# The first two attention units loaded as 512 tokens, four to a partition, and the start of the kernel put in another order

## The chip, the cores and the metric

The kernel runs on one core of one Trainium2 chip. The metric is the device time of one execution in microseconds; smaller is better. Each kernel is executed several times and the median is taken.

The engines are named as the profile names them: PE is TensorE (matmul), PEld its weight loads, DVE is VectorE, ACT is ScalarE, POOL is GpSimd, SP is SyncE. SP and POOL issue most of the transfers: those of SP are described by hardware, those of POOL by software, and POOL's can convert fp32 to fp16 on the way.

## What is computed

Attention within chunks of 64 tokens, for 8 batches, 8 heads, 576 tokens and head size 64, and then a feed-forward layer over all 4608 tokens with a gate whose steepness is a parameter:

```python
scores = scale * np.matmul(q_c, k_c.transpose(0, 1, 2, 4, 3))   # chunks of 64 tokens
scores = scores - np.max(scores, axis=-1, keepdims=True)
attn = np.exp(scores)
attn = attn / (np.sum(attn, axis=-1, keepdims=True) + 1e-09)
out = np.matmul(attn, v_c)
...
h = x @ w_in                        # x: 4608 x 512, w_in: 512 x 2048
g = h * (1.0 / (1.0 + np.exp(-beta * h)))
return (g @ w_out).astype(np.float32)   # w_out: 2048 x 512
```

The inputs are fp32 and the output is 4608 x 512 fp32. The kernel computes in fp16 with fp32 sums.

## The kernel before

**Tiling.** The tokens are cut into 18 units of 256 tokens; two units make a block of 512 tokens, so there are nine blocks. Attention goes unit by unit, the feed-forward layer block by block.

**Attention of one unit.** `load_unit` (L115) loads q and k with two neighbouring tokens to a partition (`load_qk`, L88, runs of 512 bytes in memory) and v with one token to a partition (`load_v`, L108). `emit_T` (L142) transposes 32x32 squares of q and k on DVE for the first eight units; later units use a transposing transfer on SP. `emit_sc` (L209) makes the scores, transposed, into a PSUM tile of two banks from the pool `ps_s`, and takes their exp on ACT into `et`. `emit_pv` (L247) multiplies with v, to which a column of ones is attached, so that the sum of the exps comes out as column 64; its two halves s = 0, 1 (128 tokens each) go to a tile of two banks of `ps_x` and one of `ps_s`. `emit_norm` (L264) divides by that sum on DVE and gives `x16`. `emit_xt_pe` (L282) transposes x16 on PE into PSUM and copies it on ACT to `xt`, for units 0 to 5; later units use a transfer (`emit_xt_dma`).

**Feed-forward.** `emit_m` (L296) makes h for 128 of the 2048 hidden columns m: four matmuls into one bank of `ps_p` (a ring of four one-bank buffers), a tanh with beta/2 as its scale on ACT, and one instruction on DVE that gives the gated value `gt`. With the argument 256 it does half of a block's tokens. `emit_t` (L329) multiplies gt with w_out for 128 tokens, in pieces of 16 steps, copies the sum out on ACT and stores it through SP. The pools `ps_p`, `ps_s` and `ps_x` (L51 to L53) fill the eight banks: four, two and two.

**Order.** The order on each engine is the order in which the program emits instructions (`manual_schedule`, L354). Every engine works its own list in order and waits at an instruction until its operands are there.

**The start.** Unit 0 is split by heads: heads 0 to 3 (a = 0) are loaded by SP as fp32 (`raw0`) and converted on ACT (q) and DVE (k); heads 4 to 7 (a = 1) are loaded by POOL with conversion (`qk0[1]`). `emit_T_half` (L171) and `emit_sc_half` (L184) transpose and score each half; the exp stands at the end of the latter. Unit 1 takes the ordinary path: `load_qk(1)` at L367, `emit_T(1)` at L390, `emit_sc(1)` at L391. POOL issues, in this order: heads 4 to 7 of unit 0, q and k of unit 1, four tiles of v, eight groups of w_in (256 hidden columns each, L372), three of w_out, then unit 2, the last of w_out, and further units.

Between the steps `emit_idle` (L349) puts matmuls on a zero tile whose result nobody reads ("warm" in the profile): 11, 3, 13, 4, 3, 3 and 2 of them, each 512 columns wide. From L405 the layer begins for the first half of block 0 (unit 0's tokens), with the PE transposes of unit 1 between its steps; L417 does the second half (unit 1's tokens).

**Later parts that the change touches.** Units 2 and 3 are worked beside the second product of block 0 (L422 to L441), unit 4 near the end of the first product of block 1, and units 5 to 7 beside the second product of block 1 (L459 to L479). In `emit_xt_pe` the half s = 0 goes to a tile of `ps_x`; s = 1 goes to `ps_s` for unit 2 and to `ps_p` for the others.

The lines that decide where the transposes go:

```python
pool, tag = (ps_x, "x") if s == 0 else (ps_s, "s") if u == 2 else (ps_p, "p")
xp = pool.tile([128, 4, 128], FP16, tag=tag, name="xp")
```

The softmax here doesn't subtract the row's maximum and nothing guards it: scores larger than these inputs give would overflow.

## Time and profile before

| | us |
|---|---|
| median of 3 runs | 292.15 (291.8 to 292.45) |
| the profiled execution | 291.74 |
| its span, first to last instruction | 290.0 |
| PE busy in the span | 283.1 (98%) |
| PE busy with filler matmuls (39) | 11.2 |
| ACT, DVE, POOL busy | 146.0, 139.8, 97.5 |
| granted TensorE clock, mean | 1.00 |

The profiled execution lasts 1.74 us longer than its span; what lies before the first and after the last instruction is not in the span. A matmul of 512 columns in the long unbroken stretches takes 0.216 us. The matmul durations in the groups are longer (about 0.37 us), because neighbouring matmuls overlap and their ends are modelled; so the distance between starts is what counts.

In the profile's lists each line gives the start in microseconds, the duration, the engine, the line of the program, and the operation with output and input; in square brackets stands the idle time of the engine just before, and what ended it. The chain of waits follows the work that ended last back from the end, at each step to what released it. In the list of stretches each engine's busy time is followed by its number of instructions, and the last two numbers are the share of the DMA engines and the GB/s written.

The time of a transfer is given from its issue to its landing. The DMA engines are busy for over 90% of every slice from 2.5 us to about 100 us.

### The profile page before, as it was taken

To read this page: it belongs to the slowest core of one execution; us is meant where nothing else is said; L and a number is where in the kernel's file an instruction comes from. 1 tells how busy PE (TensorE), PEld (TensorE's weight loads), DVE (VectorE), ACT (ScalarE), POOL (GpSimd) and SP (SyncE) were. 2 spreads that over 40 slices of the span, in tenths; PEclk is the share of its full clock that TensorE was granted. 3 is DMA by queue.
4 is the path that set the end of the run, shared out by engine and by line. 5 is a ranking of instruction groups with operands and counts; after the bars stand their busy time and mean duration, and the time that the engine had idled before them with its cause. 6 is when DMAs were issued, how large, how long until landed. Compare 5 with 4: busy or idle time off the path is not lost.

```text
span 290.0 us, 6476 instructions
## 1 busy us (share of the span) xinstructions
PE 283.1 (98%) x2695; PEld 135.5 (47%) x2695; DVE 139.8 (48%) x252; ACT 146.0 (50%) x224; POOL 97.5 (34%) x126
## 2 busy tenths in 40 slices
PE   7999999999999999999999999999999999999995
PEld 2464445545544444444444444444444444444444
DVE  3477444687366644534454444445453636433300
ACT  3277318783456645454545554455445544444411
POOL 8864569379152985070717070000000000000000
PEclk9999999999999999999999999999999999999999
DMA  9999999999969999999999999946346202100111
GB/s 143 170 196 205 177 176 212 211 161 158 133 98 135 200 168 144 168 151 156 135 123 171 118 158 113 198 65 92 91 107 78 75 36 72 38 36 36 38 72 72
DMA packets 141932, 36.86 MB, mean 127 GB/s; under 512 B 130000, under 2 KB 137424, under 8 KB 141904
## 3 DMA queue, kind: packets, MB, share of 16 engines
q0 software_dynamic: 101216, 18.10, 84.2%
q1 hardware_dynamic: 40544, 18.24, 34.4%
q8 instruction: 21, 0.34, 0.5%
q10 hardware_dynamic: 144, 0.13, 0.1%
q14 instruction: 7, 0.06, 0.1%
HBM read 36.71 MB, written 9.44 MB: 159 GB/s over the span
## 4 chain that ended last, share of the span: by engine, by line
PE 91%; DMA 2%; ACT 2%; DVE 2%; POOL 1%; issue 1%; DVEq 0%; ACTq 0%; POOLq 0%
PE hps L303 43%; PE ops L335 41%; DMA ku<-in_k_dram 2%; PE x L256 2%; PE sc L231 2%; PE sc L218 1%; PE ops L540 1%; ACT xt L288 1%; DVE x L271 1%; ACT sg L313 1%; PE warm L352 1%; POOL h L360 1%; PE xp L287 1%; DVE kT L154 0%; ACT osb L345 0%
## 5 line engine op out<-in xcount | busy, mean ns | idle before, releaser
L317 DVE SCALAR_TENSOR_TENSOR gt<-sg,hps 128x512 f16<-128x512 f32 (+1 forms) x152 | 99.2, 658 | 114.5 <-ACT sg L313 114.4
L313 ACT ACTIVATE sg<-hps,beta 128x512 f32<-128x512 f32 (+1 forms) x152 | 100.4, 665 | 74.7 <-PE hps L303 74.7
L303 PE MATMUL hps<-xt,win 128*128 128x512 f16 (+1 forms) x608 | 136.7, 368 | 0.4 <-ACT xt L288 0.2
L335 PE MATMUL ops<-wout,gt 128*128 128x512 f16 x560 | 131.1, 379 | 0.0
L303 PEld LDWEIGHTS <-win 128*128 128x128 f16 x608 | 57.6, 98 | 61.8 <-issue 0.9
L335 PEld LDWEIGHTS <-gt 128*128 128x128 f16 x560 | 53.8, 98 | 63.3
L345 ACT ACTIVATE osb<-ops 128x512 f32<-128x512 f32 x35 | 20.9, 598 | 44.4 <-PE ops L335 44.4
L110 POOL DMA_DIRECT2D vbig<-in_v_dram x40 | 34.2, 876 | 10.0 <-DMA wout<-in_moe_w_out_dram 4.3
L96 POOL DMA_DIRECT2D qu<-in_q_dram x22 | 18.7, 860 | 41.5 <-DMA qT<-qu 39.0
L271 DVE TENSOR_TENSOR x<-x,rd 128x512 f16<-128x512 f32 (+1 forms) x40 | 25.2, 637 | 1.4
L96 POOL DMA_DIRECT2D ku<-in_k_dram x22 | 18.8, 876 | 0.4 <-DMA ku<-in_k_dram 0.4
L240 ACT ACTIVATE et<-sc 128x1024 f16<-128x1024 f32 (+1 forms) x9 | 7.4, 834 | 10.2 <-PE sc L231 10.2
L352 PE MATMUL warm<-idle 128*128 128x512 f16 x39 | 11.2, 429 | 1.2 <-DVE braw L356 1.2
L267 DVE RECIPROCAL rd<-x 128x8 f32<-128x8 f32 x36 | 7.2, 200 | 8.8 <-PE x L256 8.8
L224 ACT ACTIVATE et<-sc 128x1024 f16<-128x1024 f32 x10 | 10.2, 1015 | 0.0
L256 PEld LDWEIGHTS <-et 64*64 64x64 f16 x576 | 6.1, 107 | 7.4 <-issue 3.8
L102 POOL DMA_DIRECT2D ku<-in_k_dram x10 | 7.7, 772 | 2.5 <-DMA win<-in_moe_w_in_dram 1.3
L102 POOL DMA_DIRECT2D qu<-in_q_dram x10 | 7.7, 781 | 2.4 <-DMA win<-in_moe_w_in_dram 1.4
L288 ACT COPY xt<-xp 128x512 f16<-128x512 f16 x12 | 6.7, 588 | 3.3 <-PE xp L287 3.3
L256 PE MATMUL x<-vbig,et 64*64 64x65 f16 x576 | 8.1, 195 | 0.0
L154 DVE STREAM_TRANSPOSE kT<-ku 128x512 f32<-128x512 f32 x7 | 5.0, 711 | 4.9 <-DMA ku<-in_k_dram 4.9
L553 DVE TENSOR_SCALAR osb<-ops 128x256 f32<-128x256 f32 x1 | 0.4, 424 | 12.5 <-PE ops L540 12.5
(34 smaller groups left out, 60.2 us busy)
## 6 DMA issues: line engine op xcount, KB each, us to landing
out_dram<-osb SPq DMA_DIRECT2D x35, 256.0 KB, 3.2
vbig<-in_v_dram POOLq DMA_DIRECT2D x32, 128.0 KB, 7.9
qu<-in_q_dram POOLq DMA_DIRECT2D x20, 128.0 KB, 6.6
ku<-in_k_dram POOLq DMA_DIRECT2D x20, 128.0 KB, 8.2
win<-in_moe_w_in_dram POOLq DMA_DIRECT2D x8, 256.0 KB, 9.2
wout<-in_moe_w_out_dram POOLq DMA_DIRECT2D x4, 512.0 KB, 12.2
qu<-in_q_dram POOLq DMA_DIRECT2D x4, 256.0 KB, 6.5
ku<-in_k_dram POOLq DMA_DIRECT2D x4, 256.0 KB, 7.3
```

What stands on the lines that cost most here:

```text
L96: nc.gpsimd.dma_start(out=tv[off:off + n, sp], in_=src[b, :, s:s + n, :].rearrange("h p d -> p h d"),)
L102: nc.gpsimd.dma_start(out=t[off // 2:(off + n) // 2], in_=src[b, :, s:s + n, :].rearrange("h (p r) d -> p h r d", r=2),)
L110: nc.gpsimd.dma_start(out=vbig[off:off + n, i, :, 0:D], in_=v[b, :, s:s + n, :].rearrange("h p d -> p h d"),)
L224: nc.scalar.activation(out=et, in_=sc, func=ACTF.Exp, scale=scale)
L256: nc.tensor.matmul(out=x[64 * c:64 * c + 64, r, g, 0:D + 1], lhsT=(et[64 * r:64 * r + 64, s, 4 * c + g, :] if u < XU else et[64 * r:64 * r ...
L271: nc.vector.tensor_tensor(out=o, in0=x[:, r, :, 0:D], in1=rd[:, r].to_broadcast(list(o.shape)), op=ALU.mult)
L303: nc.tensor.matmul(out=hps[:, 0:n], lhsT=w_in16[m // 2][:, kk, (m % 2) * 128:(m % 2) * 128 + 128], rhs=xr[:, c0 // CH:(c0 + n) // CH, 2 * ...
L313: nc.scalar.activation(out=sg[:, 0:n], in_=hps[:, 0:n], func=ACTF.Tanh, scale=beta2[:, m:m + 1])
L317: nc.vector.scalar_tensor_tensor(out=gt_t[j][:, m, c0:c0 + n], in0=sg[:, 0:n], scalar=1.0, in1=hps[:, 0:n], op0=ALU.add, op1=ALU.mult,)
L335: nc.tensor.matmul(out=ops, lhsT=gt_t[j][:, kk, t * 128:(t + 1) * 128], rhs=w_out16[kk // 4][:, kk % 4, :], start=(kk == 0), stop=(kk == K ...
L345: nc.scalar.activation(out=osb, in_=ops, func=ACTF.Copy, scale=0.5)
L352: nc.tensor.matmul(out=d[:, 0:w], lhsT=idle[:, 0:128], rhs=idle[:, 0:w])
```

## The change

The change has these parts:

- **Loads.** The tiles `raw0`, `qk0` and `qkT0` now hold 512 tokens of four heads, four neighbouring tokens to a partition: units 0 and 1 together. Each of the four transfers covers twice the bytes in runs of 1024 bytes. `load_qk(1)` and `emit_T(1)` are gone.
- **Conversion.** For the first half both q and k are converted on ACT.
- **Scores.** `emit_sc_half(u, a)` makes the scores of one unit and one half of the heads; the exp is a function of its own, `emit_ex_half`. Unit 1's scores go to a tile of `ps_x`. All scores that remain after the first half of unit 0 are emitted in one stretch, and unit 1's exp covers all its heads.
- **PV.** Both units' products follow each other. The second half of each goes to two one-bank tiles of `ps_p`; its norm then has two reciprocals and two multiplications, while the other halves have one of each.
- **PE transposes.** For unit 0's and unit 1's s = 0 they use `ps_s` and `ps_x`; for units 2 to 5 both halves go to one tile of `ps_x`, each in a bank of its own.
- **Order of the start.** The filler is 26 and 6 matmuls, and none later. beta is scaled after the norms. The transposes of unit 1 and the first m steps are interleaved in another way, with s = 1 of unit 1 first.
- **Order in block 1.** Unit 4's norms come ahead of `emit_T(5)`. `emit_t(1, 1, 0, 8)` comes ahead of `emit_sc(5)`, and `emit_t(1, 1, 8)` ahead of `emit_pv(5)`.

```diff
-    raw0 = [const.tile([128, HH, 2, D], FP32, name=f"raw{i}") for i in range(2)]
-    qk0 = [[const.tile([128, HH, 2, D], FP16, name=f"h0{i}{a}") for i in range(2)] for a in range(2)]
-    qkT0 = [[const.tile([128, HH, CH, 2], FP16, name=f"t0{i}{a}") for i in range(2)] for a in range(2)]
+    raw0 = [const.tile([128, HH, 4, D], FP32, name=f"raw{i}") for i in range(2)]
+    qk0 = [[const.tile([128, HH, 4, D], FP16, name=f"h0{i}{a}") for i in range(2)] for a in range(2)]
+    qkT0 = [[const.tile([128, HH, 128, 2], FP16, name=f"t0{i}{a}") for i in range(2)] for a in range(2)]
...
     def emit_T_half(a):
-        if a == 0:
-            nc.scalar.copy(out=qk0[a][0], in_=raw0[0])
         for i in (0, 1):
-            if a == 0 and i == 1:
-                nc.vector.tensor_copy(out=qk0[a][1], in_=raw0[1])
+            if a == 0:
+                nc.scalar.copy(out=qk0[a][i], in_=raw0[i])
             nc.vector.transpose(
...
-    def emit_sc_half(a):
+    def emit_sc_half(u, a):
         if a == 0:
-            et_t[0] = et_p.tile([128, 2, H, CH], FP16, tag="et", name="et")
-            x_t["s0"] = ps_s.tile([128, 2, H, CH], FP32, tag="s", name="sc")
-        sc = x_t["s0"]
+            et_t[u] = et_p.tile([128, 2, H, CH], FP16, tag="et", name="et")
+            pool, tag = ((ps_s, "s"), (ps_x, "x"))[u]
+            x_t["sc", u] = pool.tile([128, 2, H, CH], FP32, tag=tag, name="sc")
+        sc = x_t["sc", u]
         qt, kt = qkT0[a]
         for h in range(HH):
             for e in range(2):
-                for c in range(4):
...
+                for s in range(2):
+                    p0 = 64 * u + 32 * s
+                    for c in range(2):
+                        nc.tensor.matmul(
+                            out=sc[64 * c:64 * c + 64, s, HH * a + h, :],
+                            lhsT=kt[p0:p0 + 32, h, 64 * c:64 * c + 64, e],
+                            rhs=qt[p0:p0 + 32, h, 64 * c:64 * c + 64, e],
...
+    def emit_ex_half(u, a, n=1):
+        hs = slice(HH * a, HH * (a + n))
+        nc.scalar.activation(
+            out=et_t[u][:, :, hs], in_=x_t["sc", u][:, :, hs], func=ACTF.Exp, scale=scale)
...
-    def emit_pv(u):
+    def emit_pv(u, where=("x", "s")):
...
+            if where[s] == "p":
+                x = [ps_p.tile([128, 4, 128], FP32, tag="p", name=f"y{r}") for r in range(2)]
+            else:
+                pool = {"x": ps_x, "s": ps_s}[where[s]]
+                x = [pool.tile([128, 2, 4, 128], FP32, tag=where[s], name="x")]
...
-        nc.vector.reciprocal(out=rd, in_=x[:, :, :, D:D + 1])
-        for r in ([0, 1] if u < 2 else [slice(0, 2)]):
+        for r, z in [(slice(0, 2), x[0])] if len(x) == 1 else list(enumerate(x)):
+            nc.vector.reciprocal(out=rd[:, r], in_=z[..., D:D + 1])
...
-        pool, tag = (ps_x, "x") if s == 0 else (ps_s, "s") if u == 2 else (ps_p, "p")
-        xp = pool.tile([128, 4, 128], FP16, tag=tag, name="xp")
+        if u < 2 and s == 1:
+            xp = ps_p.tile([128, 4, 128], FP16, tag="p", name="xp")
+        else:
+            if u not in xp_t:
+                pool, tag = ((ps_s, "s"), (ps_x, "x"))[u > 0]
+                xp_t[u] = pool.tile([128, 2, 8, 128], FP16, tag=tag, name="xp")
+            xp = xp_t[u][:, s, 0:4]
...
-                    in_=src[0, HH * a:HH * a + HH, 0:UNIT, :].rearrange("h (p r) d -> p h r d", r=2),
+                    in_=src[0, HH * a:HH * a + HH, 0:2 * UNIT, :].rearrange("h (p r) d -> p h r d", r=4),
...
-        load_qk(1)
...
-        emit_idle(11, 512)
+        emit_idle(26, 512)
         emit_T_half(0)
-        emit_sc_half(0)
-        emit_idle(3, 512)
+        emit_sc_half(0, 0)
+        emit_ex_half(0, 0)
+        emit_idle(6, 512)
         emit_T_half(1)
-        emit_sc_half(1)
+        emit_sc_half(0, 1)
+        emit_ex_half(0, 1)
+        emit_sc_half(1, 0)
+        emit_sc_half(1, 1)
+        emit_ex_half(1, 0, 2)
         nc.vector.transpose(out=bt, in_=braw)
-        nc.scalar.activation(out=beta2, in_=bt[:, 0:KFF], func=ACTF.Copy, scale=0.5)
-        loads_to(4)
-        emit_idle(13, 512)
-        emit_T(1, ("qT", "kT"))
-        emit_sc(1)
         loads_to(5)
-        emit_idle(4, 512)
-        emit_pv(0)
+        emit_pv(0, ("s", "p"))
         emit_norm(0, 0)
         emit_norm(0, 1)
-        emit_idle(3, 512)
+        emit_pv(1, ("x", "p"))
+        emit_norm(1, 1)
+        emit_norm(1, 0)
+        nc.scalar.activation(out=beta2, in_=bt[:, 0:KFF], func=ACTF.Copy, scale=0.5)
         emit_xt_pe(0, 0)
-        emit_idle(3, 512)
         emit_xt_pe(0, 1)
-        emit_idle(2, 512)
-        emit_pv(1)
-        emit_norm(1, 0)
-        emit_norm(1, 1)
         a0, v0 = emit_m(0, 0, 0, 256, True)
         a1, v1 = emit_m(0, 1, 0, 256, True)
         a0()
+        emit_xt_pe(1, 1)
         a1()
+        a2, v2 = emit_m(0, 2, 0, 256, True)
         emit_xt_pe(1, 0)
+        a2()
         v0()
         v1()
-        a0, v0 = emit_m(0, 2, 0, 256, True)
-        a0()
-        emit_xt_pe(1, 1)
-        v0()
+        v2()
         emit_m(0, 3, 0, 256)
...
         emit_pv(4)
-        emit_T(5)
         emit_norm(4, 0)
         emit_norm(4, 1)
+        emit_T(5)
         emit_T(6)
         emit_t(1, 0, 8)
         emit_xt_pe(4, 0)
         emit_xt_pe(4, 1)
+        emit_t(1, 1, 0, 8)
         emit_sc(5)
-        emit_t(1, 1, 0, 8)
+        emit_t(1, 1, 8)
         emit_pv(5)
         emit_norm(5, 0)
         emit_norm(5, 1)
         emit_T(7)
-        emit_t(1, 1, 8)
         emit_t(1, 2, 0, 8)
```

## The prediction

> **What bounds the kernel now.** I read the page first: TensorE is busy 98% of a 290.0 us span at full clock, and its chain is 91% TensorE, so a change can only gain where TensorE waits or runs filler. The table by stretches says where that is: from 80 us on nothing idles except at the very end.

> ```profile
> 10.00:14.00 4.00, 3.79 (x108) 1.75 (x105) 1.71 (x5) 1.02 (x1) 3.29 (x5) 1.00 2.04 173
> 14.00:19.00 5.00, 4.84 (x69) 3.17 (x70) 3.67 (x12) 3.43 (x8) 3.11 (x5) 1.00 1.46 199
> 80.00:290.00 210.00, 206.68 (x1660) 95.96 (x1657) 95.50 (x161) 102.91 (x152) 45.41 (x56) 1.00 1.01 109
> ```

> The chain of waits of the first 40 us names what sets the start. The reader is to see that unit 1's k, the fourth transfer on the POOL queue, holds everything until 10.2 us, that a zigzag of small steps follows, and that TensorE runs without a break only from 19.00, when the last of the four copies of transposed x is out.

> ```profile
> 2.89 0.85 POOL qu L102
> 3.74 6.45 DMA ku<-in_k_dram
> ...
> 16.09 0.56 PE hps L303 x4
> ...
> 16.74 0.84 ACT sg L313 x2
> 17.59 0.51 ACT xt L288
> 18.10 0.23 ACT sg L313
> ...
> 18.36 0.60 ACT xt L288
> ...
> 19.00 12.27 PE hps L303 x64
> ```

> The timeline of TensorE gives later gaps. The scores of unit 3 could start at 44.86 (four matmuls of 0.216 us from 44.00) and start at 45.37, held by the copy that frees their PSUM tile: 0.51 us. The second transpose of unit 4 could start at 68.36 and starts at 68.73, since VectorE does T(5) ahead of the norms: 0.37 us.

> ```profile
> 45.37 0.70 PE L231 MATMUL sc<-qT,kT 32*64 32x64 f16 x64 [0.34 <-ACT xt L288]
> 68.73 0.40 PE L287 MATMUL xp<-ident,x 128*128 128x128 f16 x4 [0.21 <-DVE x L271]
> ```

> Last, the transfers. DMA is saturated from 2.5 us on, and the first weights only just make it: w_in group 0, issued 8.80, lands 7.2 later at 16.0, and m=0 starts at 16.03; group 1 lands at 17.3 and m=2 starts at 17.33; the fourth v tile lands 7.2 after 7.4, at 14.6 (the last number of a line is the time to landing).

> ```profile
> vbig<-in_v_dram POOLq DMA_DIRECT2D x1, 128.0 KB, 7.2
> win<-in_moe_w_in_dram POOLq DMA_DIRECT2D x1, 256.0 KB, 7.2
> win<-in_moe_w_in_dram POOLq DMA_DIRECT2D x1, 256.0 KB, 7.7
> ```

> How fast small runs move, in four stretches of half a microsecond:

> ```profile
> DMA packets 325, 0.16 MB, mean 329 GB/s; under 512 B 4, under 2 KB 325, under 8 KB 325
> DMA packets 341, 0.09 MB, mean 174 GB/s; under 512 B 341, under 2 KB 341, under 8 KB 341
> DMA packets 614, 0.08 MB, mean 155 GB/s; under 512 B 614, under 2 KB 614, under 8 KB 614
> DMA packets 196, 0.10 MB, mean 197 GB/s; under 512 B 4, under 2 KB 196, under 8 KB 196
> ```

> They start at 3.0 (raw, 512 B written fp32), 6.5 (q, k cast, 512 B read), 10.5 (v, 256 B read) and 17.0 (w_in, 1 KB read): 650, 682, 1,228 and 392 packets a microsecond.

> [...] read side, 314 GB/s at 256 B, 349 at 512 B, 401 at 1 KB. [...] The trace shows the two queues overlapping only for some 0.5 us near 3.7. [...] Here filler matmuls are 0.427 us apart at first (weight loads at 1.59 to 4.15) and 0.2155 later; 11 took 4.12 us, so some 8.3 were cold. [...]

> **Part by part.** *Transfers.* Four q, k transfers of 512 B runs for unit 0 plus two for unit 1 become four of 1 KB runs. Bytes are the same. Before: 1,024 raw packets / 650 = 1.58 us, 3,072 cast / 640 (mean of 310 to 341 per half) = 4.80, 4,096 v / 1,228 = 3.34; sum 9.72. After: 1,024 raw of 1 KB and 1,024 cast of 1 KB read, both taken at w_in's 392, 2.61 each, and v 3.34: 8.56. So v's end and all weights come **1.15 us** earlier. Raw at 1 KB isn't in the trace: if a packet costs what a 512 B one does it takes 1.58, if twice, 3.15, so 0.6 to 2.2 us. POOL also issues two transfers fewer (1.8 us), never the bound here.

> *Unit 0's first half.* Raw q would land near 4.0 and raw k between 5.3 and 6.3 (alone or sharing the engines). ScalarE now casts both: 128x1024 as the exp of that size, 1.02 us. k's cast to 7.3, its VectorE transpose of 128x512, 0.71: 8.05. Filler: 8.3 x 0.427 + 17.7 x 0.2155 + 1.19 = 8.55. So the filler decides; sc(0,0) runs at 8.55 (0.37, half of 0.71), six more (1.29) to 10.21. Second-half transposes (2 x 0.71, k landing about 8.5) end at 9.5: covered.

> *Scores, exps, PV.* Three halves from 10.21, the last starting at 10.95. An exp starts 0.51 after its half (5.69 to 6.20): ex(0,1) 10.72 to 11.32, ex(1) 11.46 to 12.48. PV(0) at 11.38. A norm's pitch is 0.84 unsplit (67.12 to 67.96) and 1.16 with four instructions (2 x 0.24 + 2 x 0.34): norm(0,0) 11.65 to 12.5, norm(0,1) to 13.65, norm(1,1) to 14.8, norm(1,0) to 15.65. PV(1) needs ex(1) and v tile 3, which lands at 14.6 - 1.15 = 13.45: it ends at 13.65, and on TensorE both transposes of unit 0 are queued behind it. They run at 13.65 and 13.88; a copy starts 0.43 after its transposes (14.02 to 14.45), pitch 0.49, ending 14.66 and 15.15; **m=0 at 15.19** (weights: 16.0 - 1.15 = 14.85). beta2 (0.21) moves into ScalarE's wait for these transposes: nothing.

> *To the steady stretch.* From m=0: tanh after 0.65 to 1.1, copy(1,1) from 1.29 (TensorE: m=0, m=1, transposes), tanh at 1.79, copy(1,0) at 2.2 to 2.8, m's second half at **2.84** after m=0. Before it was 19.00 - 16.06 = 2.94. So the steady stretch starts at 18.03: **0.97 us gained**. Bounds: with v early enough m=0 waits for weights at 14.85 and 1.3 is gained; with no earlier transfer PV(1) waits until 14.6 and m=0 is at 16.3, about 0.2 lost.

> *Later.* Unit 2's second transpose leaves sc(3)'s tile alone: 0.51 comes free, but ScalarE's row of exps, osb and tanh behind it moves only about 0.4 (osb before the exps ends at 45.8): **0.4**. norm before T(5): x16(4,1) is ready at 68.05, before 68.36: **0.37**. T(5) ends at 69.4; sc(5) now follows t(1,1,0,8), at 70.3: covered. PV(5) to its transposes has 1.73 us of matmuls for two norms of 0.84: just covered, 0.1 at stake. The six loads of unit 9 that T(5) releases on POOL go 2.4 us later in the order; unit 9's transposes are past 84 us. The loads of units 2 to 5 keep their order; T(2)'s k lands at 35.9, sc(2) is at 38.10 with 0.75 to spare, and both move by about 1. That units 3 to 5 leave one bank of the four-bank ring free costs nothing: their next user of ps_x is over 1.4 us away.

> *Sum*: 0.97 + 0.4 + 0.37 = 1.75. The profiled execution took 291.74 (span 290.0 and 1.74 around), so 290.0; the median, 292.15, is 0.41 above, so **290.4**.

> **Rivals.** *Only the later gaps* (0.20): the start stays at 19.0 because the clock is released late or transfers come no earlier. For it: filler is a fixed count; each microsecond longer cold adds 0.5 us to its end, which decides by 8.55 against 8.05. Against: 1 KB runs do move more. 292.15 - 0.8 = 291.4. *PV(1) ahead of the transposes* (0.10): v tile 3 lands last among stragglers (two v tiles landed 7.7 and 7.2 after issue, the first two 6.4 and 6.2); if it doesn't move and the weights lag as well, the start loses 0.4 to 0.8: 292.0. *The clock falls* (0.15), the other side: between 10.2 and 15.2 the change leaves only three halves of scores, two PV (0.38 each) and two transposes, some 2.3 us of TensorE work, where now filler takes some 2.6 us of 10.98 to 15.7. For it: every window of the kernel before holds filler or dense work, so the trace excludes nothing. Against: no gap alone exceeds some 2 us. The price is half of the cold time on work that TensorE limits: [...] take 2.5: 292.15 - 1.75 + 2.5 = 292.9. It decides from 3.5 us cold.

> **How the numbers follow.** The forecast has 0.55: 290.4, own range 289.5 to 291.2. A measurement here can't tell less than 0.2%, 0.6 us, from nothing. Faster: 0.55 + 0.17 of the first rival = 0.72; same: 0.03 + 0.08 + 0.02 = 0.13; slower: 0.15. Range 289.3 to 291.9, which leaves out most of the clock rival and some of the v one.

> **What would show it.** Right: hps unbroken from 17.6 to 18.4; last v about 13.4, w_in 0 about 14.9; first scores near 8.55, behind filler; no wait at sc(3) or in unit 4's transposes. Wrong: hps at 0.43 us per 512 columns after 15 us; m=0 waiting for a DMA; first scores waiting for raw k; a new wait at sc(2).

## The result, and the profile after

| | before | after |
|---|---|---|
| median, us | 292.08 (6 runs) | 298.72 (297.61 to 298.77, 6 runs) |
| profiled execution, us | 291.74 | 297.61 |
| its span, us | 290.0 | 295.8 |
| mean granted TensorE clock | 1.000 | 0.988 |

The ratio of after to before is 1.022, with an interval of 1.0204 to 1.0236: the changed kernel is slower by some 6.6 us, where a gain of 1.75 had been forecast.

The chain of waits of the first 23 us of the changed kernel (start, length, what):

```profile
1.19 7.26 PE warm L366 x26
8.45 0.38 PE sc L194 x31
8.83 1.40 PE warm L366 x6
10.23 0.46 PE sc L194 x33
...
10.71 1.59 ACT et L204 x2
...
12.34 0.32 PE x L262 x16
12.66 0.12 PE y L262 x15
12.79 3.76 issue
16.55 0.26 PE y L262
16.81 0.56 PE xp L301 x4
...
17.39 1.08 ACT xt L302 x2
...
18.51 1.87 PE hps L317 x8
...
22.43 7.73 PE hps L317 x43
```

Up to 12.79 us it is nearly the predicted start: filler to 8.45 (8.55 had been worked out), the second stretch of scores at 10.20 (10.21), the exps from 10.71 (10.72). Then comes a line that has no counterpart before: 3.76 us of "issue", in which TensorE waits for nothing that the profile shows, between the 15th and the 16th of sixteen like matmuls of PV(1). It is one head's product like those ahead of it, with operands that were ready for them as well, and the profile names no releaser for it. m=0 starts at 18.51 and the steady stretch at 22.43, against 19.00 before.

The stretches of the changed kernel (from:to and its length, then the busy time of PE, PEld, DVE, ACT and POOL, the granted clock, the DMA share and GB/s):

```profile
12.00:13.00 1.00, 0.44 (x31) 0.33 (x31) 0.97 (x3) 0.40 (x2) 0.89 (x2) 1.00 1.45 195
13.00:14.00 1.00, 0.00 (x0) 0.00 (x0) 0.93 (x5) 0.00 (x0) 0.37 (x2) 1.00 1.45 197
14.00:15.00 1.00, 0.00 (x0) 0.00 (x0) 0.31 (x1) 0.00 (x0) 0.55 (x1) 0.72 1.44 203
15.00:16.00 1.00, 0.00 (x0) 0.00 (x0) 0.00 (x0) 0.00 (x0) 0.00 (x0) 0.50 1.47 192
18.00:19.00 1.00, 0.49 (x3) 0.36 (x3) 0.33 (x1) 0.46 (x1) 0.42 (x2) 0.50 1.45 196
```

The clock, the first number after the engines, falls to half within the stand (at 14.4 us) and is still there when m=0 begins. It is back at 1.00 from about 21.3 us.

The totals of TensorE's waits after, and the two later transposes that the prediction spoke of, from its timeline:

```profile
PE y L262 <- issue: 3.8, 1, 3.8
PE xp L301 <- ACT xt L302: 2.8, 4, 0.9
PE hps L317 <- ACT xt L302: 1.2, 3, 0.7
```

```profile
48.31 0.38 PE L301 MATMUL xp<-ident,x 128*128 128x128 f16 x4 [0.94 <-ACT xt L302]
73.79 0.38 PE L301 MATMUL xp<-ident,x 128*128 128x128 f16 x4 [0.94 <-ACT xt L302]
```

The second line of the totals is new too: four times the second transpose of a unit (2, 3, 4 and 5) waits until ScalarE has copied the first one out. The copy sits behind other ScalarE work; the chain of the changed kernel shows how that reaches the end of the execution:

```profile
47.18 0.60 ACT osb L359
47.78 0.49 ACT xt L302
48.27 0.04 issue
48.31 0.38 PE xp L301 x4
```

The increase of 5.8 us in the span can be read off the starts of the same work in both timelines: 3.43 us are there at the steady stretch (22.43 against 19.00); sc(3) is 0.68 further behind (49.48 against 45.37), the next long stretch 0.22 (55.68 against 51.35), and sc(6) 1.54 (81.79 against 75.92). The sum is 5.87. After that nothing is added.

**What the stand is.** Both pages have a row for a DMA queue of another kind, which carries 21 blocks of 16 KB. The list of the transfers of the changed kernel in the quarter microsecond from 14.0 shows one of them, alone among the loads:

```profile
q0 software_dynamic: 98, 0.05, 140.2%
q8 instruction: 1, 0.02, 23.7%
```

TensorE has 2,688 matmuls and as many weight loads: 5,376 instructions, 21 times 256. That fits blocks of 256 instructions, 128 matmuls with their weight loads; all_fixes, below, shows two stands 128 matmuls apart. The 3.76 us stand before the 224th matmul (26 + 32 + 6 + 96 + 32 + 31 = 223 come first). Counted back by 128, the block ahead of it begins with the 96th. From the starts of the matmuls that is at 10.5 us after and at 11.0 before; the 224th is due at 12.8 after and at about 15.8 before, within PV(1). The block's packet begins between 12.0 and 12.25 in the kernel before. With the 2.4 us that lie between packet and restart after (14.1 to 16.55) it would be usable at about 14.5: some 1.3 us in hand, which no view of the kernel before shows as a wait.

No trace shows the moment at which a block is asked for, only when its packet begins. Late in the changed kernel the last packet of this queue begins at 281.5 us, the only one of any queue from 281 to 282, while the matmul that begins the block ahead, the 2,656th by the count, starts only at 288.7, 33 matmuls on. In all the kernels of this document one packet is 36 matmuls ahead of that mark and none of the others more than 34. From this comes an estimate: the block is asked for about 33 matmuls ahead of that mark, here at the 63rd: the fifth of six fillers after, at 9.6 us, and the 17th of 32 scores before, at 7.7. The timelines of after (first line) and before:

```profile
8.76 1.47 PE L366 MATMUL warm<-idle 128*128 128x512 f16 x6
7.51 0.45 PE L194 MATMUL sc<-t,t 32*64 32x64 f16 x32 [0.61 <-DVE t L177]
15.65 0.45 PE L256 MATMUL x<-vbig,et 64*64 64x65 f16 x32
```

Counted from there the packet begins 4.5 us later in both kernels. What differs is the time until the 224th matmul is due: 8.1 us before, 3.2 after.

### The profile page after: what moved, and what is told of

It reads as the page before. It is cut to its first block, busy times and chain, and to the rows that moved or that the text cites. A ratio compares the mean times of both kernels' runs of the same rounds, so it can differ in the third digit from the quotient of the medians.

```text
span 295.8 us, 6460 instructions
## 1 busy us (share of the span) xinstructions
PE 282.7 (96%) x2688; PEld 136.4 (46%) x2688; DVE 140.3 (47%) x249; ACT 148.0 (50%) x225; POOL 95.6 (32%) x124
## 4 chain that ended last, share of the span: by engine, by line
PE 94%; ACT 3%; issue 2%; DVE 0%; DVEq 0%
PE hps L317 43%; PE ops L349 41%; PE warm L366 3%; PE x L262 2%; ACT xt L302 2%; PE sc L234 1%; PE sc L221 1%; PE ops L550 1%; PE xp L301 1%; ACT osb L359 1%; ACT et L204 1%; PE sc L194 0%; DVE osb L563 0%; PE y L262 0%; ACT sg L327 0%
## 5 line engine op out<-in xcount | busy, mean ns | idle before, releaser
L317 PEld LDWEIGHTS <-win 128*128 128x128 f16 x608 | 58.3, 99 | 63.0 <-issue 1.9
L96 POOL DMA_DIRECT2D qu<-in_q_dram x22 | 18.7, 858 | 48.5 <-DMA qT<-qu 38.8
L278 DVE TENSOR_TENSOR x<-x,rd 128x512 f16<-128x512 f32 x34 | 23.5, 692 | 1.3
L96 POOL DMA_DIRECT2D ku<-in_k_dram x22 | 18.8, 874 | 0.0
L243 ACT ACTIVATE et<-sc 128x1024 f16<-128x1024 f32 (+1 forms) x8 | 6.4, 809 | 8.9 <-PE sc L234 8.7
L366 PE MATMUL warm<-idle 128*128 128x512 f16 x32 | 8.7, 435 | 1.2 <-DVE braw L370 1.2
L301 PE MATMUL xp<-ident,x 128*128 128x128 f16 x48 | 5.1, 242 | 3.0 <-ACT xt L302 2.8
L102 POOL DMA_DIRECT2D ku<-in_k_dram x9 | 6.8, 752 | 2.7 <-DMA win<-in_moe_w_in_dram 1.5
L102 POOL DMA_DIRECT2D qu<-in_q_dram x9 | 6.8, 762 | 2.3 <-DMA win<-in_moe_w_in_dram 1.3
L563 DVE TENSOR_SCALAR osb<-ops 128x256 f32<-128x256 f32 x1 | 0.4, 425 | 12.5 <-PE ops L550 12.5
## 6 DMA issues: line engine op xcount, KB each, us to landing
out_dram<-osb SPq DMA_DIRECT2D x35, 256.0 KB, 3.3
vbig<-in_v_dram POOLq DMA_DIRECT2D x32, 128.0 KB, 7.5
qu<-in_q_dram POOLq DMA_DIRECT2D x20, 128.0 KB, 6.0
ku<-in_k_dram POOLq DMA_DIRECT2D x20, 128.0 KB, 8.1
win<-in_moe_w_in_dram POOLq DMA_DIRECT2D x8, 256.0 KB, 9.7
qu<-in_q_dram POOLq DMA_DIRECT2D x3, 256.0 KB, 7.1
ku<-in_k_dram POOLq DMA_DIRECT2D x3, 256.0 KB, 7.8
```

The costliest lines, as they stand in the source:

```text
L96: nc.gpsimd.dma_start(out=tv[off:off + n, sp], in_=src[b, :, s:s + n, :].rearrange("h p d -> p h d"),)
L102: nc.gpsimd.dma_start(out=t[off // 2:(off + n) // 2], in_=src[b, :, s:s + n, :].rearrange("h (p r) d -> p h r d", r=2),)
L278: nc.vector.tensor_tensor(out=o, in0=z[..., 0:D], in1=rd[:, r].to_broadcast(list(o.shape)), op=ALU.mult)
L317: nc.tensor.matmul(out=hps[:, 0:n], lhsT=w_in16[m // 2][:, kk, (m % 2) * 128:(m % 2) * 128 + 128], rhs=xr[:, c0 // CH:(c0 + n) // CH, 2 * ...
L366: nc.tensor.matmul(out=d[:, 0:w], lhsT=idle[:, 0:128], rhs=idle[:, 0:w])
```

## The experiments

Two theories were set out for the start, where TensorE's stop of 3.76 us is called the stand. The first: the stand is the instruction block, late since the DMA engines are saturated (a share of 1.44 to 1.47 in the stretches above from 12 to 19 us), and the half clock follows from the stand. The rival: sparse work on TensorE lets the clock fall by itself, whatever the stand. For the later 2.8 us: the shared tile of the transposes, or the order of block 1.

**The later waits alone.** In the changed kernel, the transposes of units 2 to 5 get separate tiles, as before:

```diff
+        elif u >= 2:
+            pool, tag = (ps_x, "x") if s == 0 else (ps_s, "s") if u == 2 else (ps_p, "p")
+            xp = pool.tile([128, 4, 128], FP16, tag=tag, name="xp")
```

> The transposes of units 2 to 5 go back to separate PSUM tiles; all else is the changed kernel. Theory (the program itself makes the second half's transposes wait for ScalarE's copy of the first half, because both halves are in one tile): the four waits of TensorE on that copy (0.94, 0.24, 0.94, 0.67 us by the profile) go, the wait of unit 3's scores (0.51) comes back, unit 4's norm order keeps its 0.37: about 2.8 us less than the changed kernel, 295.9. Rival (the copies are late for a reason of ScalarE's own): the waits stay and the time is within 0.5 us of the changed kernel's 298.7.

295.61 us, ratio 1.0122 (1.0097 to 1.0148): 3.1 below after, or 2.9 by the distances of both to the kernel before that ran beside them. The four waits are gone from the totals:

```profile
PE y L262 <- issue: 3.3, 1, 3.3
...
PE x L262 <- ACT et L204: 0.7, 2, 0.5
PE sc L234 <- ACT xt L305: 0.3, 1, 0.3
```

and the wait of sc(3) for a copy (last line) is back. So the shared tile cost some 3 us, though its halves lie in separate banks. What makes the second transpose wait is then the program's own dependence between the two halves and not the banks; order_two_banks, below, tests this with the same two banks.

**Does the stand belong to a place or to a count?** The changed kernel, with 20 more matmuls in the first filler at about the same length:

```diff
-        emit_idle(26, 512)
+        emit_idle(8, 512, 38, 240)
```

(8 of 512 columns, then 38 of 240.)

> The first filler is 8 matmuls of 512 columns and 38 of 240 instead of 26 of 512: the same TensorE time, 20 matmuls more. Theory (TensorE runs out of instructions: the stall belongs to a place in the instruction list, the 447th instruction): the 3.8 us stall moves 20 matmuls forward, to the 12th matmul of PV(1), inside its first half, and begins within 0.2 us of where PV(1) begins; time unchanged within 0.6 us (298.7). Rival (the last matmul of PV(1) waits for its data, v or exps): the stall stays at the last matmul of PV(1).

298.71 us, ratio 1.0228 (1.0206 to 1.025). The timeline of this kernel:

```profile
13.63 0.28 PE L262 MATMUL x<-vbig,et 64*64 64x65 f16 x11 [0.54 <-ACT et L204]
16.79 0.25 PE L262 MATMUL x<-vbig,et 64*64 64x65 f16 x5 [2.88 <-issue]
```

The stand has moved by 20 matmuls, into the middle of another group: 46 + 32 + 6 + 96 + 32 + 11 = 223 come before it, as in after. It belongs to the count.

**The block's transfer.** The changed kernel, with w_in and all later loads held back on POOL until DVE has transposed beta, at some 10 us:

```diff
         nc.vector.transpose(out=bt, in_=braw)
+        nc.gpsimd.tensor_copy(out=gate, in_=bt[:, 0:1])
+        make_identity(nc, ident)
+        for g in range(8):
+            load_w_in(g)
...
```

> POOL holds back every w_in, w_out and later transfer until VectorE has transposed beta (10.2 us in the changed kernel), by one small copy; before it only v is queued. Theory (the block of instructions [...] stands behind the long transfers of w_in): [...] the stall of 3.8 us shrinks to under 1, w_in group 0 lands at about 14, the steady stretch begins at 18 to 18.5 instead of 22.4 and the time is about 294.5. Rival (the sparse work alone drops the clock): the stall shrinks, but the clock still falls to half between 14 and 18 and at least 1.5 us of the gain is missing, 296 or more. Rival (the stall isn't about instructions): it stays, and with w_in later the time is 298.7 or more.

295.97 us, ratio 1.0138 (1.0113 to 1.0162): 2.75 below after. The stretches show the DMA engines quieter:

```profile
12.00:13.00 1.00, 0.46 (x36) 0.35 (x37) 0.61 (x2) 1.00 (x2) 1.00 (x2) 1.00 0.71 79
15.00:16.00 1.00, 0.36 (x7) 0.24 (x5) 0.93 (x4) 0.83 (x2) 1.00 (x3) 0.90 1.06 112
16.00:17.00 1.00, 0.70 (x4) 0.50 (x4) 0.33 (x1) 0.25 (x1) 1.00 (x3) 0.50 1.41 172
```

The block's packet began between 11.75 and 12.0, and the stand shrank to 1.18 us, at the same matmul; under 1 us had been expected. Counted from the 63rd matmul (10.3 us here), the packet begins after 1.5 us and the block is usable after 4.3, against 4.5 and 6.9 in the changed kernel. So its transfer does contend with the loads. The clock still fell, at 15.8 us, and the time is almost that of the rival, 296 or more.

**The order of block 1 alone,** in the kernel before:

```diff
         emit_pv(4)
-        emit_T(5)
         emit_norm(4, 0)
         emit_norm(4, 1)
+        emit_T(5)
...
-        emit_sc(5)
         emit_t(1, 1, 0, 8)
+        emit_sc(5)
+        emit_t(1, 1, 8)
...
-        emit_t(1, 1, 8)
```

> The kernel before with the new order of block 1 alone: unit 4's norms ahead of T(5), t(1,1) around sc(5). Theory (my term of 0.37 us holds): the gap before unit 4's second transpose goes and the time is 291.7, a ratio of about 0.9988. Rival (the gap moves on to another wait of the same stretch): ratio 1.000 within its interval.

291.40 us over 22 runs, ratio 0.9982 (0.9974 to 0.999). It gains 0.5 us, near the 0.37 expected; in its timeline both transposes of unit 4 stand as one group of eight at 68.25, with no wait.

**The boundary elsewhere.** The changed kernel with 126 matmuls of 104 columns as first filler, so that the 224th matmul, with which the third block of the expectation begins, falls among the scores:

```diff
-        emit_idle(26, 512)
+        emit_idle(126, 104)
```

> The changed kernel with the first filler as 126 matmuls of 104 columns instead of 26 of 512: about the same TensorE time, 100 matmuls (200 instructions) more[...]. Theory (the stall is the third block coming too late): no stall of over 1 us in TensorE between 9 and 18 us, time about 295.5 (295.0 to 296.2, the clock still falling because TensorE has little to do from 11 to 15), 294.5 if the clock stays up. Rival (the stall belongs to PV(1) or to the transfers): it stays and the time is 298.7.

296.45 us, ratio 1.0156 (1.0142 to 1.0171), against the 295.5 expected. That no stand of over 1 us would be left failed: one of 1.53 us stands ahead of the last 37 scores, again after 223 matmuls. None is left at PV(1). The clock is below 1.00 from 17.0 to 20.4 us. It stayed up at the end of the stand and fell 3.4 us later, with no wait above 0.76 us in between.

**More filler in the gaps,** without touching the stand: two 512-column matmuls ahead of PV(1) and four ahead of m=0 in the changed kernel.

```diff
+        emit_idle(2, 512, d6)
...
-        a0, v0 = emit_m(0, 0, 0, 256, True)
+        a0, v0 = emit_m(0, 0, 0, 256, True, 4)
```

> The changed kernel with six filler matmuls in the gaps: two ahead of PV(1), four ahead of m=0, in tiles that are there anyway. Theory (the stall for instructions keeps TensorE empty for over 3 us, and filler behind it can't prevent that the clock falls): time within 0.6 us of 298.7, clock at half from about 14.6 to 21. Rival (sparse work, not the stall, is what drops the clock): the clock stays up or comes back by 18 us, at least 1 us less.

298.36 us, ratio 1.0227 (1.0209 to 1.0245): nothing gained. The stand stays (3.59 us, again after 223 matmuls), and the clock falls near its end, at 16.9 us.

**Three repairs together:** separate tiles, the boundary among the scores, and the six fillers.

```diff
-        emit_idle(26, 512)
+        emit_idle(120, 110)
```

> All three causes taken away together: transposes of units 2 to 5 in separate tiles, first filler as 120 matmuls of 110 columns, and the six filler matmuls in the gaps. Theory (instructions, clock and the shared tile are the whole loss): no stall, clock at 1.0 after its first release, steady stretch from 17.7 to 19.0 depending on when the clock is first released, a later gain of 0.37; 291.4, from 290.6 to 292.0. Rival (something else in the new start costs as well): over 292.5.

292.96 us, ratio 1.0039 (1.0024 to 1.0054). Of the 6.6 us 5.8 are gone; the rest, 1.05 us above the kernel before that ran beside it, is above the expectation. The timeline shows what is left at the start:

```profile
10.88 0.74 PE L194 MATMUL sc<-t,t 32*64 32x64 f16 x65 [0.68 <-DVE bt L409]
12.63 0.45 PE L194 MATMUL sc<-t,t 32*64 32x64 f16 x31 [1.01 <-issue]
```

a stand of 1.01 us, and a clock below 1.00 from 14.1 to 17.5. That the clock is the whole rest is not shown: one of the six executions had a mean clock of 1.000 and took 293.47 us, as long as the longest of the others.

**A repair of both transposes.** The kernel before with the order of block 1 as above and unit 2's two transposes in the two banks of one tile, but both emitted ahead of both copies:

```diff
+    def emit_xt_two(u):
+        xp = ps_x.tile([128, 2, 8, 128], FP16, tag="x", name="xp")
+        for s in range(2):
+            xf = x16_t.pop((u, s)).rearrange("p r h d -> p (r h d)")
+            for g in range(4):
+                nc.tensor.transpose(out=xp[:, s, g, :], in_=xf[:, g * 128:(g + 1) * 128], identity=ident)
+        for s in range(2):
+            nc.scalar.copy(out=xt_at(u, s), in_=xp[:, s, 0:4])
...
-                emit_xt_pe(2, 0)
-                emit_xt_pe(2, 1)
+                emit_xt_two(2)
```

> The kernel before with the new order of block 1, and unit 2's two transposes in the two banks of one tile of ps_x, but both transposes emitted ahead of both copies, so that the program puts no wait of the second transposes on the first copy. Theory (the idea of two banks was sound and its order made the wait): TensorE doesn't wait between the two transposes, unit 3's scores don't wait for the copy, another 0.4 us beside the 0.5 that the order alone gave: 291.0, ratio 0.9968. Rival (the gap turns up again at the scores' exps or at unit 3's transposes): ratio as with the order alone, 0.998.

291.04 us over 22 runs, ratio 0.9972 (0.9963 to 0.998). This is the lowest ratio measured, and it beats both kernels; its interval overlaps with those of order_only and order_thin. Both transposes run as one group, and sc(3) waits for no copy of a transpose:

```profile
44.00 0.61 PE L295 MATMUL xp<-ident,x 128*128 128x128 f16 x8
44.45 1.03 PE L344 MATMUL ops<-wout,gt 128*128 128x512 f16 x4
45.40 0.71 PE L231 MATMUL sc<-qT,kT 32*64 32x64 f16 x64
```

This execution reached the transposes 0.44 us later than the kernel before (44.00 against 43.56 in its timeline), and sc(3) only 0.03 later (45.40 against 45.37): from the one to the other 1.40 us instead of 1.81, with the same eight transposes and four matmuls between.

**The clock, without a stand.** The kernel before with its last 12 fillers only 16 columns wide. The count of instructions, and so the boundary, is as before.

```diff
-        emit_idle(4, 512)
+        emit_idle(4, 16)
...
-        emit_idle(2, 512)
+        emit_idle(2, 16)
```

> The kernel before with the last 12 filler matmuls (4, 3, 3, 2) 16 columns wide instead of 512: the number of instructions and their order are those of before, so the instruction block is asked for and needed as there and no stall of TensorE for it should appear. From 11.7 to 16.0 us TensorE then has some 1.2 us of work in 4.3. Theory (sparse work alone, without any stall, lets the clock fall): the clock is below 1.00 for about 3 us or more from about 15 to 16 us, and the time is 1 to 2 us above before, 293.0 to 294.0. Rival (the clock fell in the changed kernel only because of the gap of 3.8 us): the clock stays at 1.00, and the time is that of before within 0.3 us.

291.41 us, ratio 0.9989 (0.9976 to 1.0002). The rival was expected to show here, and in the profiled execution it did not: the clock is at 1.00 throughout, though TensorE is idle for a third of 11.8 to 15.2 us:

```profile
11.80:15.20 3.40, 2.18 (x84) 1.71 (x81) 2.21 (x8) 2.15 (x3) 2.97 (x5) 1.00 1.70 182
```

Its longest wait there is 0.70 us. But four of the twelve executions have a mean clock of 0.994, and they are the four slowest (292.04 to 292.62 us, the others 290.84 to 291.56). Half clock for 3.4 us in 290 gives just that mean. All 101 executions of the kernel before that ran beside the experiments have 0.998 or more. So the clock can fall with this filler gone, in a third of the executions; whether a longer wait went with it there is not recorded.

The same with the 13 fillers ahead of unit 1's scores thinned as well:

```diff
-        emit_idle(13, 512)
+        emit_idle(13, 16)
```

> As before_thin, with the 13 filler matmuls ahead of unit 1's scores thinned too, so that from 8.3 to 16.0 us TensorE has some 1.9 us of work in 7.7, with its longest gap about 2.6 us. Theory: the clock is below 1.00 from 12 to 13 us at the latest, and the time is 1.5 to 2.5 us above before, 293.5 to 294.5; what is cold before 16 us costs little, since TensorE waits there. Rival: the clock stays at 1.00 and the time is that of before within 0.3 us.

292.66 us, ratio 1.0017 (1.0006 to 1.0028). Here TensorE stands 2.33 us for a transpose of k, which is a plain wait for data, and the clock falls at 10.2 us and stays at half until 20.4. Some 10 us at half clock go with only 0.7 us in the median; m=0 waits for w_in until 15.61 in any case. That the clock falls beside a plain wait for data as it does beside the stand is what this run adds.

**Both gains together.** order_two_banks with the last 12 fillers thinned:

```diff
-        emit_idle(4, 512)
+        emit_idle(4, 16)
...
```

> order_two_banks with the last 12 filler matmuls (4, 3, 3, 2) 16 columns wide, as in before_thin. There the steady stretch started at 18.13 us instead of 19.00 at full clock, and the median was 0.57 below before, with an interval that just touched 1. If the two gains add, 290.2 to 290.8 (ratio 0.994 to 0.997), below order_two_banks by 0.3 to 0.8. Rival (the late filler costs nothing in the median, since other waits take its place): the ratio of order_two_banks, 0.997, with nothing added.

291.29 us, ratio 0.9978 (0.9962 to 0.9994): nothing added. In the profiled execution TensorE waited 0.91 us for w_in at 15.57, and the clock fell at about 16 us. Of the fourteen executions, six have a mean clock of 1.000 and take 290.15 to 291.18 us, most of them in the range that was expected (290.2 to 290.8) or just under it; the eight others take 291.12 to 293.02. The late filler of the kernel before guards against such executions.

**All repairs of the start,** boundary_fill with 145 fillers of 90 columns and the loads held back:

```diff
-        emit_idle(120, 110)
+        emit_idle(145, 90)
```

> boundary_fill with the first filler cut into 145 matmuls of 90 columns instead of 120 of 110, and with the loads of w_in, w_out and later units held on POOL until the transpose of beta, as in win_late. [...] Theory (a stall or gap of 1 us or more is what lets the clock fall; sparse work with gaps of at most 0.7 us did not in before_thin): no stall over 0.5 us, the clock stays at 1.00, and the time is 291.0 to 291.8, not distinguishable from before. Rival (the clock falls from sparse work whatever the stall): it is below 1.00 for some 3 us from about 14 us, and the time is 292.5 to 293.2.

295.96 us, ratio 1.0144 (1.0127 to 1.0161). Both expectations failed, for a reason that confirms the count:

```profile
12.11 0.64 PE L194 MATMUL sc<-t,t 32*64 32x64 f16 x56 [1.17 <-issue]
...
14.26 0.75 PE L304 MATMUL xp<-ident,x 128*128 128x128 f16 x6
16.79 0.40 PE L304 MATMUL xp<-ident,x 128*128 128x128 f16 x2 [1.78 <-DVE rd L276]
```

The first stand comes after 145 + 32 + 6 + 40 = 223 matmuls, the second after 351, exactly 128 further: the 25 fillers added had drawn the next boundary into the start too. The profile puts the second down to VectorE, but the reciprocal it names (16.10 in VectorE's timeline) belongs to a later norm; what the last two transposes read was done at 15.08. A packet of the instruction queue ran between 14.25 and 14.5, some 2.4 us before TensorE went on. As this kernel has a second stand, it doesn't tell whether the change would be level with before without any.

## Why the prediction was wrong

**The step that failed first** is "PV(1) needs ex(1) and v tile 3, which lands at 14.6 - 1.15 = 13.45: it ends at 13.65". The list of what PV(1) needs left out its own instructions. It ended at 16.8. m=0, put at 15.19, came at 18.51: 3.32 us, more than the whole forecast gain. The cover was lost by the change itself: it took out the filler and put 64 short PV matmuls directly behind 96 short score matmuls, so that the 128 matmuls from the 96th to the 224th took 2.3 us instead of 4.8, and the 161 from the estimated asking 3.2 instead of 8.1. The block takes 6.9 us from there beside busy DMA engines (4.5 to its packet, 2.4 to the restart). The count (filler_shift, boundary, all_fixes) and the contention (win_late) are shown; the moment of asking is an estimate, and how long a block takes with no other transfer at all was not measured.

**The clock.** The rival "the clock falls" named the symptom, and its reason, too little work on TensorE, is borne out in part. The sentence "no gap alone exceeds some 2 us" was true of the gaps that had been worked out, and the stand made one of 3.76. Half clock made the way from m=0 to the steady stretch 3.92 us instead of 2.84: 1.08. A long gap is not needed, though, as the clock records of the traces show. In nine kernels the clock falls 10.24 us after it was first granted in full, and in before_thin25 3.41 after it; half clock lasts 3.41, 6.83 or 10.24 us (in after it is full from 4.20 us and half from 14.44 to 21.27). All are multiples of 3.41, wherever the stand lies. These lines show the last stretch of 3.41 us ahead of the fall in after, one in before_thin that no fall followed, and two of boundary, of which the first has the stand and the second the fall at its end:

```profile
11.03:14.44 3.41, 1.06 (x84) 0.82 (x71) 2.44 (x8) 1.36 (x3) 2.58 (x4) 1.00 1.60 195
10.36:13.77 3.41, 2.50 (x113) 1.70 (x110) 2.06 (x6) 1.12 (x2) 3.41 (x5) 1.00 2.11 169
10.19:13.60 3.41, 1.95 (x65) 0.96 (x64) 0.32 (x2) 1.19 (x2) 2.43 (x4) 1.00 1.89 181
13.60:17.02 3.42, 2.13 (x109) 1.55 (x109) 2.42 (x9) 1.87 (x4) 2.22 (x3) 1.00 1.45 195
```

In the ten kernels whose clock fell, TensorE was busy for 0.44 to 2.20 us of the stretch of 3.41 us ahead of the fall. Of such stretches at full clock in the first 24 us that no fall followed, all have 2.41 us or more but the one of boundary with 1.95. So the busy time alone does not settle it; what does was not shown, nor whether the clock of the changed kernel would have stayed up without its stand. The rival's price, 2.5, was the author's estimate for cold matmuls at 15 us, and missed the stand itself.

So the steady stretch came 4.40 us after the 18.03 that was forecast: 3.32 + 1.08.

**Later.** The term for unit 2, "Unit 2's second transpose leaves sc(3)'s tile alone: 0.51 comes free", failed. That two banks of one tile need no wait for each other was the author's estimate; the wait comes from the tile: with one tile and the order transpose, copy, transpose, copy, the second transpose waits for the first copy, 0.94 us at unit 2. It cost 3.1 us (own_banks), and with the order turned, the gain seems to come: order_two_banks is 0.36 us below order_only, where 0.4 had been forecast. Their intervals overlap, but the traces have the 0.41 us too (1.40 against 1.81). "norm before T(5)", 0.37, was right in mechanism and size: 0.5 with order_only, which has the new order around sc(5) too, with an interval of 0.3 to 0.8 us.

**The sum.** The three terms of the forecast make 1.74 and not 1.75, which changes nothing. The profiled execution was forecast at 290.0 and took 297.61. Of these 7.6 us the start has 4.40, and what comes after it 3.2: 0.77 of gains that did not show, and 2.4 added (0.68 + 0.22 + 1.54).

**What was right.** The transfers moved the way it said, and further: v tile 3 landed at about 12.3 (13.45 forecast) and w_in 0 at about 13.5 (14.85). "If a packet costs what a 512 B one does" is nearest to it. As neither was waited for in the end, nothing came of it. The filler deciding the first scores was right too, but 8.55 is one execution's value: the first filler ended at 8.45 in the profile after, at 9.77 in filler_shift and 9.67 in own_banks, where full clock was first granted at 4.2, 6.9 and 6.7 us. The median of after lies 1.1 us above its profiled execution, which such a spread can explain; the kernel before hides its first filler behind loads: its first scores (5.69 in its timeline) wait another 0.38 us for a transpose on VectorE.

## What to carry to other kernels

When many short matmuls are drawn together, look where a block of TensorE's instructions ends. In these kernels the stands come after 223 and 351 matmuls, 128 apart, but not at multiples of 128 from the start; a stand or a shifted count has to find the first. Then compare the time from some 33 matmuls ahead of one boundary (the estimate above) up to the next with that of a block of instructions beside the loads that run then: 3.2 us with 6.9 in the changed kernel. A wait put down to "issue" between two like matmuls is the sign (3.76 us in after), and a shift of the count the test (20 matmuls in filler_shift, and the stand again after 223). Before two halves of a PSUM tile are counted as independent, look at the order in which their writers and readers are emitted: both writers first, then both readers (the second transpose of unit 2 waited 0.94 us in after, and not at all in order_two_banks). In the sparse start of these kernels the clock stayed up with filler between the steps: it fell in none of the 101 executions of the kernel before, and with the last 12 fillers thinned in four of twelve (before_thin) and eight of fourteen (order_thin). One profiled execution at full clock doesn't show that it stays up in the others.
